# Adaptive layer norm, attention and GEGLU on one core: early bank sharing, the last eight heads as one unit, evictions as tasks, inverse roots on GpSimd

## The chip, the cores and the metric

The kernel runs on one core of a Trainium2 chip. The metric is device time of one execution in microseconds. A core has five engines that run at the same time, each with its own queue of instructions, and meet only at semaphores: TensorE (PE, matrix multiplication; PEld is its loading of weights), VectorE (DVE), ScalarE (ACT, activation functions), GpSimd (POOL) and SyncE (SP, which issues the transfers here). Matrix products land in PSUM, eight banks of 512 fp32 columns in 128 partitions; everything else on chip lies in SBUF.

## The reference

One transformer block: 2048 tokens of 512 numbers, 32 heads of 16, a feed-forward part of 1792, all in bf16. Six vectors (shift, scale and gate of both halves) come from a small vector c.

```python
mod = (silu(c) @ w_mod).reshape(1, 6, 1, -1)
sa, ca, ga, sb, cb, gb = ...
h = layernorm(x) * (1 + ca) + sa
q, k, v = heads of h @ wqkv
p = softmax(q k^T / 4)
x = x + ga * ((p v) @ wo)
h = layernorm(x) * (1 + cb) + sb
x = x + gb * ((gelu(h @ w_gate) * (h @ w_up)) @ w_down)
```

layernorm divides by sqrt(v + 1e-5); gelu is the tanh form.

## The kernel before

**Scores and exponentials.** Scores are computed transposed, keys in the partitions and queries in the columns. A *unit* is a group of heads for one set of query tokens; a *round* of a unit gives four score banks (one for each of four heads, or head pairs), and all banks of all rounds make one long sequence of 2048 positions. `ps_sc` has six banks (`self.scp`), used as two halves of three (CH = 3): even chunks take banks 0 to 2, odd chunks banks 3 to 5. One ACT instruction takes the exponential of the whole chunk (line 1485). In place of the exponential of a bank, DVE can make it by bit arithmetic (`bits`, line 1307): one instruction per bank writes 16-bit patterns, and after four banks of a round (a *quad*) a task of three passes over 128x2048 elements finishes them (`power_task`, line 1574: `mant`, `square`, `expo`). The exponentials are multiplied by V with a column of ones beside it (`pv_mms`), into the one bank `ps_pv`; while the second unit runs (the first two units go through the keys together), bank 5 of `ps_sc` is its accumulator, and odd chunks then have two banks.

**The order is made by a planner.** The Python program records all instructions in one list (`_Recorder.rec`), with a model of when each engine is free, and adds the semaphores. `stream` is a loop that decides at each step what PE does next: a chunk of scores, a round of PV, a step of *side* work, or filler. Sharing a chunk (line 1467) means that one of its three banks goes to DVE; it is allowed if DVE is free early enough (`rule.early`), if a quad can be opened (`new_quad`: two free buffers, not more than `rule.back` waiting DVE steps, V there), and after the keys of group 2 are there. A chunk may also go to DVE entirely (`rule.alone`, line 1449). RULES has a row of nine limits for every 64 positions of the sequence (`SEGB`): ready, hole, back, fill, lag, early, alone, ahead, side2.

**Side work** runs between the chunks: projections of K, Q and V, later for each set of tokens the output projection (`side_wo`), layer norm, and the feed-forward part (`side_ffn`). Each piece fills a bank (`ps_mi`, or bank 5) and is then evicted by DVE. Work on DVE that need not come at once is a *task*: a list of steps under a key, run when the model has DVE free, in the order of `urgency`.

**Units and sets.** The 2048 queries are cut into SETS of 512, 512, 256, 256, 256, 128 and 128 tokens. The first two sets have units of four heads, the later ones of eight heads (n = 2, two heads for each of four row groups). APART names head groups of the last two sets that stay single: for the last set, groups 6 and 7 are two units of four heads and 128 columns. PEN names units whose end is made on DVE alone, without transfers: transposition of 32x32 blocks, reciprocal of the sums, a product, and transposition back (`unit_end`, line 1626).

**Prologue.** `prologue` (line 593) loads x and w_mod, takes mean and variance of four tiles of 128 tokens (tile 1 on ACT), and finds 1/sqrt(v + eps) in eight DVE steps (`ln_rstd_step`: an estimate by integer arithmetic and two Newton steps). Between them DVE makes `sc_bf`, the right operand of the modulation matmuls (`mod_cols`). Then come the norms, PE's transposes, the modulation, the first projections, and the first exponential. POOL makes constants and fills `vaug` (the ones) and `rb`.

**Tail.** The last two sets overlap with the end of attention. For the set before the last, `side_raw` computes gate and up projections in eight chunks (`raw_chunk`), each copied raw out of PSUM by DVE; after the last exponential `tail_rest` applies gelu, product and down projection. `tail_end` does output projection, statistics, inverse root (`ln2_steps`, here six DVE steps), norm, transposes and the feed-forward part of the last tile.

Of the kernel before, what the change touches and what calls it, by code (L numbers as in the profile page):

```python
# [7 lines left out]
ALU = mybir.AluOpType  # L8
# [6 lines left out]
P = 128  # L15
# [18 lines left out]
PEN = {NSET - 2: (6,), NSET - 1: (4, 6, 7)}  # L34
APART = {NSET - 2: (), NSET - 1: (6, 7)}
# [18 lines left out]
def WIN(ends):  # L54
# [8 lines left out]
URGENT = 12  # L63
WUP, WDOWN, WWO, JOIN = (), (), (), 4
# [442 lines left out]
class _Kernel(_Recorder):  # L507
# [12 lines left out]
    def alloc(self):  # L520
# [57 lines left out]
        self.modB = sb("modB", [P, 8], FP32)  # L578
        self.rm4 = self.den[:, 0, 0:4]
# [13 lines left out]
    def prologue(self):  # L593
# [27 lines left out]
        self.memset(pool, self.rm4, Q_SCALE)  # L621
        self.affine_select(self.rm4, [[-32, 4]], ALU.is_ge, 0.0, -16, 1)
# [3 lines left out]
        self.memset(pool, self.vaug[:, :, :].rearrange("p t (h c) -> p t h c", c=VW)[:, :, :, DH:VW], 1.0)  # L626
        self.memset(pool, self.rb[:, :], 0.0)
# [69 lines left out]
    def ln_rstd_step(self, a, b, i):  # L697
# [215 lines left out]
    def ln2_steps(self, k, src=None):  # L913
# [3 lines left out]
        if src is not None:  # L917
            dst = self.normed(k, 0)
            return steps + [lambda h=h: self.ln_norm(a, dst[:, h], src[:, h]) for h in (slice(0, 256), slice(256, D))]
# [916 lines left out]
```

## Time and profile before

| | us |
|---|---|
| median of three runs | 814.53 |
| lowest, highest | 814.52, 815.75 |
| profiled execution, its own time | 814.79 |
| span of the profile | 813.1 |

The granted PE clock is 1.00 in every stage. A profile's row of the timeline gives start, duration (of merged equal instructions together), engine, line, operation, output <- inputs, shapes and count; in brackets the idle time of the engine before it and what ended it. A row of a group gives busy time, mean duration in ns, idle time before. Rows that name L385, L404, L408, L416, L421, L425, L432, L435, L438, L447 and L450 are helpers that record every operation of a kind, so the tiles tell what is what: `E` holds exponentials, `mreg` and `dreg` (among other things) the quads of DVE, `osb` the evicted accumulator, `hreg` the norms and products of the feed-forward part, `xs` the tokens.

### The profile page before, as it was taken

What the parts mean: (1) busy time and instruction counts of PE and PEld (TensorE: products, weight loads), DVE (VectorE), ACT (ScalarE), POOL (GpSimd) and SP (SyncE); (2) the same over time, 40 slices, a digit from 0 to 9 for tenths busy, and PEclk for the clock granted to TensorE, in tenths of its full rate; (3) what the DMA queues carried; (4) which work ended last, traced back from release to release, by engine and by line L of the source; (5) the groups of instructions that cost most, each with busy time, mean ns of one, the idle gap of its engine ahead of it and who ended that gap; (6) DMA issues with size and microseconds to landing.
All of it is one profiled execution on the core that took longest, in us unless ns stands there. A gap on an engine that the chain in (4) does not pass through costs nothing.

```text
span 813.1 us, 28154 instructions
## 1 busy us (share of the span) xinstructions
PE 749.0 (92%) x12749; PEld 289.8 (36%) x12749; DVE 759.8 (93%) x1330; ACT 789.1 (97%) x741; POOL 4.6 (1%) x13
## 2 busy tenths in 40 slices
PE   7899999888898998999989999999989998999998
PEld 3333242322222222222223333333443354345476
DVE  7868999999999999999999999999999999788985
ACT  6999999999999999999999999999999999999993
POOL 2000000000000000000000000000000000000000
PEclk9999999999999999999999999999999999999999
DMA  8100000000001311110003211100554542210000
GB/s 279 60 16 19 13 10 10 10 9 5 11 6 52 95 48 35 45 44 22 16 15 100 62 48 54 48 29 16 153 165 134 167 120 78 72 25 8 20 8 15
DMA packets 70138, 43.53 MB, mean 54 GB/s; under 512 B 15233, under 2 KB 67534, under 8 KB 70018
## 3 DMA queue, kind: packets, MB, share of 16 engines
q1 hardware_dynamic: 70016, 41.73, 18.1%
q8 instruction: 100, 1.64, 0.9%
q14 instruction: 20, 0.16, 0.1%
q10 hardware_dynamic: 2, 0.00, 0.0%
HBM read 39.11 MB, written 2.60 MB: 51 GB/s over the span
## 4 chain that ended last, share of the span: by engine, by line
ACT 66%; PE 20%; DVE 12%; issue 1%; DMA 0%; DVEq 0%
ACT E L404 63%; PE ps_sc L385 10%; PE ps_mi L385 7%; DVE mreg L416 4%; PE ps_pv L385 3%; ACT hreg L404 2%; DVE dreg L416 1%; ACT L404 1%; DVE dreg L408 1%; DVE hreg L425 1%; DVE mreg L408 1%; DVE st L447 1%; DVE hreg L408 0%; DVE osb L425 0%; DVE wreg L408 0%
## 5 line engine op out<-in xcount | busy, mean ns | idle before, releaser
L404 ACT ACTIVATE E<-ps_sc 128x1024 bf16<-128x1024 f32 (+1 forms) x700 | 743.0, 1293 | 4.3 <-PE ps_sc L385 3.9
L385 PE MATMUL ps_sc<-qT,kT 32*128 32x512 bf16 (+2 forms) x2304 | 281.2, 360 | 43.8 <-ACT E L404 37.3
L416 DVE TENSOR_SCALAR mreg<-ps_sc 128x512 uint16<-128x512 f32 x288 | 192.4, 685 | 12.6 <-PE ps_sc L385 10.2
L385 PEld LDWEIGHTS ps_sc<-qT,kT 32*128 32x128 bf16 x2304 | 73.0, 91 | 271.5 <-ACT E L404 227.7
L385 PE MATMUL ps_pv<-E,vaug 128*17 128x256 bf16 (+2 forms) x2696 | 149.2, 292 | 0.1
L385 PE MATMUL ps_mi<-wreg,mreg 128*32 128x512 bf16 (+1 forms) x1760 | 102.0, 330 | 5.1 <-DVE hreg L408 1.9
L416 DVE TENSOR_SCALAR dreg<-ps_sc 128x512 uint16<-128x512 f32 x132 | 88.3, 686 | 2.1 <-PE ps_sc L385 1.1
L416 DVE TENSOR_SCALAR mreg<-mreg 128x2048 uint16<-128x2048 uint16 x113 | 76.5, 683 | 0.3
L385 PEld LDWEIGHTS ps_pv<-E,vaug 128*17 128x17 bf16 x2696 | 54.7, 90 | 59.1 <-issue 43.8
L385 PEld LDWEIGHTS ps_mi<-wreg,mreg 128*32 128x32 bf16 x1760 | 38.5, 95 | 45.0 <-issue 18.1
L385 PE MATMUL ps_pv<-mreg,vaug 128*17 128x256 bf16 (+2 forms) x900 | 49.5, 292 | 1.1 <-DVE mreg L416 0.5
L408 DVE TENSOR_TENSOR mreg<-mreg 128x2048 bf16<-128x2048 bf16 x41 | 49.7, 1212 | 0.1
L385 PE MATMUL ps_pv<-xs,nil 128*17 128x512 bf16 (+1 forms) x584 | 48.4, 375 | 1.1 <-DVE osb L425 1.1
L385 PE MATMUL ps_mi<-hreg,wreg 128*32 128x512 bf16 (+1 forms) x484 | 39.6, 384 | 2.9 <-DVE qT L416 1.6
L425 DVE CAST hreg<-ps_mi 128x512 bf16<-128x512 f32 (+1 forms) x50 | 33.7, 674 | 3.4 <-PE ps_mi L385 2.6
L408 DVE TENSOR_TENSOR dreg<-mreg,dreg 128x2048 bf16<-128x2048 bf16 x29 | 35.1, 1212 | 0.1
L385 PE MATMUL ps_mi<-wo,onorm 128*32 128x512 bf16 x448 | 33.5, 383 | 0.1
L408 DVE TENSOR_TENSOR hreg<-ps_mi,hreg 128x512 bf16<-128x512 f32 x44 | 30.2, 686 | 1.4 <-PE ps_mi L385 0.9
L416 DVE TENSOR_SCALAR dreg<-dreg 128x2048 uint16<-128x2048 uint16 x42 | 28.5, 679 | 0.0
L385 PE MATMUL ps_mi<-mreg,hreg 128*32 128x512 bf16 x352 | 28.3, 385 | 0.0
L408 DVE TENSOR_TENSOR mreg<-dreg,mreg 128x2048 bf16<-128x2048 bf16 x23 | 28.0, 1218 | 0.0
L385 PE MATMUL ps_pv<-dreg,vaug 128*17 128x256 bf16 (+2 forms) x468 | 27.3, 296 | 0.4 <-DVE dreg L408 0.2
(166 smaller groups left out, 616.5 us busy)
## 6 DMA issues: line engine op xcount, KB each, us to landing
mreg<-in_B_w_gate_dram SPq DMA_DIRECT2D x28, 256.0 KB, 3.5
mreg<-in_B_w_up_dram SPq DMA_DIRECT2D x28, 256.0 KB, 2.8
mreg<-in_B_w_down_dram SPq DMA_DIRECT2D x16, 256.0 KB, 2.8
rb<-scr_rec SPq DMA_DIRECT2D x116, 32.0 KB, 1.8
dreg<-in_B_w_down_dram SPq DMA_DIRECT2D x12, 256.0 KB, 5.1
mreg<-in_w_mod_dram SPq DMA_DIRECT2D x1, 2048.0 KB, 13.2
out_dram<-xs SPq DMA_DIRECT2D x15, 128.0 KB, 1.7
xs<-in_A_x_dram SPq DMA_DIRECT2D x3, 512.0 KB, 6.1
```

The lines of the kernel that those rows point to most:

```text
L385: return self.rec("pe", lambda e: e.matmul(out, lhsT, rhs, start=start, stop=stop, tile_position=tp), [lhsT, rhs, *after], [out], cost=(n, ...
L404: return self.rec("act", lambda e: e.activation(out, in_, func, scale=scale, **kw), rd, wr, cost=self.cost("act", out, [in_], "act") + load)
L408: return self.rec(eng, lambda e: e.tensor_tensor(out, a, b, op), [a, b], [out], cost=self.cost(eng, out, [a, b], "tt"))
L416: return self.rec(eng, lambda e: e.tensor_scalar(out, a, s1, s2, **kw), rd, [out], cost=self.cost(eng, out, [a], "ts") + (60 if len(rd) > ...
L425: return self.rec(eng, lambda e: e.tensor_copy(out, in_), [in_], [out], cost=self.cost(eng, out, [in_], "ts"))
L447: return self.rec("dve", lambda e: e.bn_stats(out, in_), [in_], [out], cost=self.cost("dve", out, [in_], "bn"))
```

## The change

Four edits of the order of work and of where it is done, and new numbers in the limits.

- Odd chunks: while bank 5 of `ps_sc` would come free more than 60 ns (by the planner's model) after bank 3 and the present time, near the end of the first two units, an odd chunk takes two banks instead of waiting for three. Up to position 128 (`ODDL`) a two-bank chunk may be shared too: one bank to ACT and one to DVE. Chunks of DVE alone keep to that number of banks.
- The last set: APART is empty, so its head groups 6 and 7 are one unit of eight heads and 256 columns, in PEN as group 6.
- The eight raw evictions become tasks of urgency 0 (`RAWU`), with at most two of them open.
- The inverse roots of the first four tiles, and of the last tile, are two instructions on GpSimd: an addition of eps and a power of -0.5, for which a small tile `mhalf` is filled. The two memsets of `vaug` and `rb` on GpSimd come after the first of these, and the two DVE steps that make `sc_bf` no longer stand between steps of the root. The loop of the tail also steps tasks of GpSimd.
- RULES: 27 of the 32 rows have other numbers.

```diff
-PEN = {NSET - 2: (6,), NSET - 1: (4, 6, 7)}
-APART = {NSET - 2: (), NSET - 1: (6, 7)}
+PEN = {NSET - 2: (6,), NSET - 1: (4, 6)}
+APART = {NSET - 2: (), NSET - 1: ()}
...
+RAWU = 0
+ODDG, ODDL = 9999, 128
+ODDE = 0
...
-    (80, 50, 10, 4200, 1536, 1100, 2500, 20, 700),
...
+    (80, 200, 10, 4200, 2560, 0, 2500, 24, 700),
...
-    (30, 200, 8, 3600, 1024, 850, 4000, 24, 3200),
...
+    (30, 200, 4, 3600, 1024, 850, 1300, 24, 700),
...
         self.memset(pool, self.rm4, Q_SCALE)
+        self.memset(pool, self.mhalf, -0.5)
...
-        self.memset(pool, self.vaug[:, :, :].rearrange("p t (h c) -> p t h c", c=VW)[:, :, :, DH:VW], 1.0)
-        self.memset(pool, self.rb[:, :], 0.0)
...
         self.warm_up(10)
-        for i in range(self.RSTD):
-            self.ln_rstd_step(0, 4, i)
-            if i == 2:
-                self.stt(self.tcol[:, :], self.tcol[:, :], 1.0, self.scp[:, 0, 0:NDC], ALU.add, ALU.mult)
-            elif i == 4:
-                self.ts(dve, self.sc_bf[:, :], self.tcol[:, :], 0.5, None, ALU.mult)
+        self.ln_rstd_pool(0, 4)
+        self.memset(pool, self.vaug[:, :, :].rearrange("p t (h c) -> p t h c", c=VW)[:, :, :, DH:VW], 1.0)
+        self.memset(pool, self.rb[:, :], 0.0)
+        self.stt(self.tcol[:, :], self.tcol[:, :], 1.0, self.scp[:, 0, 0:NDC], ALU.add, ALU.mult)
+        self.ts(dve, self.sc_bf[:, :], self.tcol[:, :], 0.5, None, ALU.mult)
...
+    def ln_rstd_pool(self, a, b):
+        x, y = self.nwx[:, a:b], self.rstd[:, a:b]
+        self.ts("pool", x, self.mv[:, a:b, 1], EPS, None, ALU.add)
+        self.tt("pool", y, x, self.mhalf[:, 0:b - a], ALU.pow)
...
+            steps = [("pool", lambda: self.ts("pool", x, self.mv[:, a:b, 1], EPS, None, ALU.add)),
+                     ("pool", lambda: self.tt("pool", y, x, self.mhalf[:, 0:1], ALU.pow))]
...
     def side_raw(self, k):
         for i in range(NRAW):
+            if i > 1:
+                yield from self.until(("raw", k, i - 2))
             f = yield from self.raw_chunk(k, i, self.bank())
-            f("dve")
-            self.done(("raw", k, i))
+            if not self.dry:
+                self.task([lambda f=f: f("dve")], ("raw", k, i))
             yield END
+        for i in range(2):
+            yield from self.until(("raw", k, NRAW - 1 - i))
...
-            mem, after = take(CH - 1 if (left[units[1]] or self.two) and c % 2 else CH)
+            nb = CH - 1 if (left[units[1]] or self.two) and c % 2 else CH
+            if nb == CH and c % 2 and pos < nsplit + 48:
+                x, y = (self.probe(lambda: self.mm(self.scp[:, i, 0:P], *filler)) for i in (SC - 1, CH))
+                if x > max(y, t) + 60:
+                    nb = CH - 1
+            mem, after = take(nb)
...
-                if len(mem) == CH and ("k", 2, 0) in self.have and self.free["dve"] < max(t + 400, self.free["act"]) + self.rule.early:
+                if (len(mem) == CH or len(mem) == nb and (pos >= ODDG or pos < ODDL)) and ("k", 2, 0) in self.have and (
+                        self.free["dve"] < max(t + 400, self.free["act"]) + self.rule.early - (CH - nb) * ODDE):
...
-                    mem, after = take(CH - 1)
+                    mem, after = take(nb - 1)
```

More of the change, by code (lines that the diff above doesn't have):

```diff
@@ L578, in alloc @@
         self.modB = sb("modB", [P, 8], FP32)
+        self.mhalf = sb("mhalf", [P, 4], FP32)[:, :]
         self.rm4 = self.den[:, 0, 0:4]
@@ L918, in ln2_steps @@
             dst = self.normed(k, 0)
+            x, y = self.nwx[:, a:b], self.rstd[:, a:b]
+            steps = [("pool", lambda: self.ts("pool", x, self.mv[:, a:b, 1], EPS, None, ALU.add)),
+                     ("pool", lambda: self.tt("pool", y, x, self.mhalf[:, 0:1], ALU.pow))]
             return steps + [lambda h=h: self.ln_norm(a, dst[:, h], src[:, h]) for h in (slice(0, 256), slice(256, D))]
@@ L1103, in urgency @@
             return -2
+        if tk[1] is not None and tk[1][0] == "raw":
+            return RAWU
         if tk[1] is None or tk[1][0] in ("st2", "ln2", "den", "onorm"):
@@ L1281, in pick @@
         def pick(q):
-            used = [seq[m][2] for m in take(CH - 1)[0]]
+            used = [seq[m][2] for m in take(nb - 1)[0]]
             return next((q["rnd"][2] + j for j in q["j"] if j not in used), None)
@@ L1450, in stream @@
                     alone = []
-                    while len(alone) < CH:
+                    while len(alone) < nb:
                         if quad is None and not new_quad(overdue()):
@@ L1472, in stream @@
                     elif new_quad(hot):
-                        mem, after = take(CH)
+                        mem, after = take(nb)
                         g = pick(quad)
                 if g is not None:
-                    mem, after = take(CH - 1)
+                    mem, after = take(nb - 1)
                 items = [(m, s0 + i) for i, m in enumerate(mem)]
@@ L1674, in tail @@
             t = self.pe_now()
-            while any(self.step(x, max(self.free[x], t) + 40) for x in ("act", "dve", "sp")):
+            while any(self.step(x, max(self.free[x], t) + 40) for x in ("act", "dve", "pool", "sp")):
                 pass
@@ L1750, in tail_end @@
         yield from self.until(("ln2", k))
-        assert not self.work
+        while self.work:
+            yield None
         for dc in range(NDC):
```

50 rows, old and new, of the table RULES are left out of this document.

## The prediction

> **What bounds the kernel now.** First the page: its span and busy line, the chain that ended last, and the groups that carry the softmax exponentials.
>
> ```profile
> span 813.1 us, 28154 instructions
> PE 749.0 (92%) x12749; PEld 289.8 (36%) x12749; DVE 759.8 (93%) x1330; ACT 789.1 (97%) x741; POOL 4.6 (1%) x13
> ...
> ACT 66%; PE 20%; DVE 12%; issue 1%; DMA 0%; DVEq 0%
> ...
> L416 DVE TENSOR_SCALAR mreg<-ps_sc 128x512 uint16<-128x512 f32 x288 | 192.4, 685 | 12.6 <-PE ps_sc L385 10.2
> ...
> L416 DVE TENSOR_SCALAR dreg<-ps_sc 128x512 uint16<-128x512 f32 x132 | 88.3, 686 | 2.1 <-PE ps_sc L385 1.1
> L416 DVE TENSOR_SCALAR mreg<-mreg 128x2048 uint16<-128x2048 uint16 x113 | 76.5, 683 | 0.3
> L408 DVE TENSOR_TENSOR mreg<-mreg 128x2048 bf16<-128x2048 bf16 x41 | 49.7, 1212 | 0.1
> ```
>
> ScalarE (ACT) is the bound, with VectorE (DVE) and TensorE (PE) close behind. The scores come as 512-column banks of PSUM: DVE turned 288 + 132 = 420 of them into powers by bit arithmetic, ACT the rest. Next the shapes of ACT's exponentials and its timeline, which merges equal work.
>
> ```profile
> L404 ACT ACTIVATE E<-ps_sc 128x1024 bf16<-128x1024 f32 x460 | 452.4, 1151 | 1.5 <-PE ps_sc L385 1.2
> L404 ACT ACTIVATE E<-ps_sc 128x1536 bf16<-128x1536 f32 x236 | 344.6, 1582 | 1.2 <-PE ps_sc L385 1.1
> ```
> ```profile
> 13.63 28.57 ACT L404 ACTIVATE E<-ps_sc 128x1536 bf16<-128x1536 f32 x25 [0.58 <-PE ps_sc L385]
> ...
> 61.91 11.47 ACT L404 ACTIVATE E<-ps_sc 128x1536 bf16<-128x1536 f32 x11 [0.53 <-PE ps_sc L385]
> 74.18 232.78 ACT L404 ACTIVATE E<-ps_sc 128x1024 bf16<-128x1024 f32 x217 [0.80 <-PE ps_sc L385]
> ...
> 792.08 1.28 ACT L404 ACT_TABLE_LOAD   x1
> ```
>
> One bank more in an ACT instruction costs 1582 - 1151 = 431 ns. From 13.63 to 792.08 ACT hardly rests; the last pause of note is the 0.80 us before 74.18. So the execution has three parts: a head of 13.6 us before the first exponential, 778 us of ACT work, and a tail of 21 us. In the middle, time is won only by banks that go from ACT to DVE or by pauses that go away. Whether DVE can take more is read from busy time by stage.
>
> ```profile
> 42.50:74.20 31.70, 29.68 (x544) 11.14 (x543) 22.47 (x40) 30.29 (x31) 0.31 (x1) 1.00 0.08 20
> 74.20:692.00 617.80, 569.03 (x9063) 200.39 (x9065) 606.95 (x990) 617.57 (x565) 0.00 (x0) 1.00 0.20 54
> 692.00:792.10 100.10, 97.60 (x2429) 50.84 (x2420) 86.12 (x161) 99.77 (x99) 0.00 (x0) 1.00 0.10 25
> ```
>
> The columns are the stretch, its length, and then busy time of PE, weight loads, DVE, ACT and POOL (GpSimd). DVE is idle 9.23 us of the first stretch, 10.85 us (1.8%) of the long second, 13.98 us of the third, where PE has only 2.50 us left. A bank on DVE costs 0.685 us for the bits and a quarter of three passes over four banks, (0.683 + 1.212 + 0.683)/4 = 0.64; together 1.33 us, for 0.43 us of ACT.
>
> **The change, part by part.**
>
> *The wait for the accumulator bank (removes a wait).* While the second unit runs, the sixth score bank is its accumulator and odd chunks have two banks. The first odd chunk after it asks for three, so all its matmuls stand behind the second copy here:
>
> ```profile
> 41.41 0.69 DVE L425 CAST kT<-ps_mi 128x512 bf16<-128x512 f32 x1 [1.57 <-PE ps_mi L385]
> ...
> 72.97 0.69 DVE L425 COPY osb<-ps_sc 128x512 f32<-128x512 f32 x1
> ```
>
> It ends at 73.66 and ACT starts 0.5 us later, after its 0.80 us pause. The new test looks when that bank comes free and takes two banks if it is late. Worth 0 to -0.8; I take -0.7, since ACT's row names this very wait. What is late next is the same bank one chunk on, after the copy has ended.
>
> *Odd chunks of two banks shared early (moves banks to DVE).* Up to position 128 such a chunk may now give one bank to DVE. Sharing still waits for the keys of group 2 (first row above, done at 42.1), so this acts in the stretch from 42.50 to 74.20. Its 9.23 us of DVE idleness hold 9.23/1.33 = 6.9 banks, or -3.0 us. The other end is above nothing: DVE also evicts the K, Q and V projections there, PE refills their one bank only after that, and a bank of bits ahead of an eviction delays it by 0.69 us; one such delay that reaches ACT gives +0.7. I take three banks, 3 x 0.43 = -1.3, under half of what the idleness holds, because PE at 29.68 of 31.70 us and the two pauses of ACT (0.53 and 0.80) show that the projections press too.
>
> *Inverse roots of the first tiles by a power on GpSimd.* Head of the kernel, rows of the timelines and of the tile that holds the first part of w_mod:
>
> ```profile
> L457 SPq DMA_DIRECT2D mreg<-in_w_mod_dram x2: 462/484/507, 1.8 to 2.3; - x2
> ...
> DMA to landing us min/median/max: 6.1/6.6/7.1
> ```
> ```profile
> 1.70 0.45 POOL L438 TENSOR_SCALAR_AFFINE_SELECT den<-den 128x4 f32<-128x4 f32 x2
> 2.08 2.27 POOL L435 MEMSET vaug<- 128x512 bf16 x1
> 6.08 0.18 DVE L450 BATCH_NORM_AGGREGATE mv<-st 128x2 f32<-128x6 f32 x1
> 7.18 0.16 DVE L416 TENSOR_SCALAR sc_bf<-tcol 128x4 bf16<-128x4 f32 x1
> 7.89 0.16 DVE L421 SCALAR_TENSOR_TENSOR nwt<-mv,rstd 128x4 f32<-128x4 f32 x1
> 7.97 1.05 DVE L416 TENSOR_SCALAR dreg<-xs,mv,rstd 128x512 bf16<-128x512 bf16 x3
> 8.05 0.54 PE L385 MATMUL ps_sc<-sc_bf,mreg 128*128 128x1 bf16 x16 [0.75 <-DVE nwt L421]
> 9.10 0.61 PE L389 MATMUL ps_sc<-ident,dreg 128*128 128x128 bf16 x8
> 57.68 0.17 DVE L435 MEMSET self<- 128x128 f32 x1
> 57.99 0.31 POOL L438 TENSOR_SCALAR_AFFINE_SELECT self<-self 128x128 f32<-128x128 f32 x1 [52.78 <-DVE self L435]
> ```
>
> Eight DVE steps fall away between 6.26 and 7.86. In their place: a hop to POOL (57.85 to 57.99: 0.14), an add, a power, a hop back. POOL's nearest rows of 128x4 take 0.45/2 = 0.23 each; the power is not in the trace. Its lower bound is 0.23; from above I use the largest POOL rate here, 2.27 us for 512 columns or 18 ns for four columns, a generous forty times over: 0.7. I take 0.4, nearer the 128x4 row because that has its shape. The norms could start near 7.2 instead of 7.97. But PE decides: its first modulation matmuls need 1.81 + 6.1 = 7.91 at the least for w_mod to land, and start at 8.05, though their other operand was ready at 7.34. From there PE works without a gap into the transposes, which need the first norm by 9.10. So the earlier root buys 0, and up to about 0.6 us of lateness would be hidden as well. The two memsets, moved behind the power, have until the first V eviction, which comes after the first exponential.
>
> [...]
>
> *Last eight heads as one unit.* The tail, with the widths that come in its place:
>
> ```profile
> 792.25 0.32 DVE L432 STREAM_TRANSPOSE osb<-ps_pv 128x128 f32<-128x128 f32 x1
> 792.68 0.85 PE L385 MATMUL ps_pv<-E,vaug 128*17 128x128 bf16 x48
> 794.03 0.32 DVE L432 STREAM_TRANSPOSE osb<-ps_pv 128x128 f32<-128x128 f32 x1 [0.47 <-PE ps_pv L385]
> 795.14 0.31 DVE L432 STREAM_TRANSPOSE onorm<-rb 128x128 bf16<-128x128 bf16 x1
> 795.97 2.75 PE L385 MATMUL ps_pv<-xs,hreg 128*128 128x512 bf16 x12
> 796.35 0.69 DVE L447 BATCH_NORM_STATS2 st<-ps_sc 128x6 f32<-128x512 f32 x1
> 797.07 0.18 DVE L450 BATCH_NORM_AGGREGATE mv<-st 128x2 f32<-128x6 f32 x1
> 798.57 0.99 DVE L416 TENSOR_SCALAR E<-ps_sc,mv,rstd 128x256 bf16<-128x256 f32 x2
> ```
> ```profile
> L432 DVE STREAM_TRANSPOSE osb<-ps_pv 128x256 f32<-128x256 f32 x2 | 0.9, 446 | 0.0
> ...
> L408 DVE TENSOR_TENSOR rb<-osb,rden 128x256 bf16<-128x256 f32 x2 | 0.8, 416 | 0.0
> ```
>
> Now the last four heads' PV matmuls begin only when the four before them have left the accumulator: out at 792.57, then 1.3 us of matmuls (48 in 0.85 us, and the DVE banks behind them) up to 794.0. In one unit all but the last round or two can run while ACT still works: last matmul near 793.0, -1.0. The chain after it gets wider: transposition 0.45 for 0.32, product 0.42 for the narrow one's 0.3, and two block transpositions of about 0.3 for one; +0.55, less the 0.39 us raw eviction that stands in it now if that has gone before. Together -0.6 to -1.0: I take -0.8. Bounds 0 (the backlog of PV stays) and -1.2.
>
> *Raw evictions as tasks.* Eight evictions are no longer forced right behind their matmuls; DVE does other work meanwhile, and PE may fill the next chunk, two at most being open. DVE's 13.98 idle microseconds before 792.10 cover them, so 0; bounds -0.4 and +0.4 (one eviction in or out of the last chain).
>
> *The last tile's root.* From 797.25 to 798.57 DVE needs 1.32 us. Instead 0.14 + 0.23 + 0.4 + 0.2 = 0.97: -0.35, between -0.5 and 0 by the bounds of the power. Nothing else waits behind it on POOL.
>
> *What PE gives back.* The fourteenth tile's down matmuls take 0.23 us each from 795.97. If the normalized last tile comes 1.15 us earlier, five of them are not done when its transposes are; PE is the bound of what follows. Some fit into the gaps around the modulation: I take back +0.4.
>
> *The planner's limits (RULES).* They change how many banks DVE takes where, no instruction's price. In the long stretch DVE idles 1.8%, so little is to be won; I take 0, bounds -2.6 and +4.4 (below).
>
> Sum: -0.7 - 1.3 - 0.8 - 0.35 + 0.4 = -2.75. The profiled execution took 814.79 us (span 813.1 and 1.7 around it), 0.26 over the median of 814.53. So 814.53 - 2.75 = **811.8 us**.
>
> **The rivals.**
>
> *The limits cost banks (slower).* Many rows are new: one stretch goes from early 1100 to 0, another's backlog limit from 8 to 4, and DVE gets a bank only when both allow. If DVE's idle share between 74.20 and 692 rose from 1.8% to 4%, that is 13.9 us, 10.4 banks, +4.4: 816.2. It decides from 2.75/0.43 x 1.33 = 8.5 us more idleness (3.1%) on. Against it: other rows raise the same limits, or lower the bar for chunks of DVE alone. Chance 0.13.
>
> *The limits win banks.* A third of the 24.8 idle microseconds after 74.20 holds 6.2 banks, -2.6: 809.2. Against it: after 692 PE is 97.5% busy. Chance 0.18.
>
> *Sharing early buys nothing*, the projections being the bound in that stretch: 811.8 + 1.3 = 813.1. For it: the pauses of ACT there. Chance 0.17.
>
> *The memsets hold the norms up.* Vaug's would run from about 7.1 to 9.4; a first norm after it ends at 9.8, 0.7 behind the transposes' 9.10, and the second memset could meet the other norms. Taking 1.0: 812.8. No SBUF-to-SBUF norm overlaps POOL in the trace, so it is neither borne out nor excluded. Chance 0.08.
>
> [...]
>
> *The power is slow.* At 2 us the tail's root takes 2.57 us for 1.32 and loses 1.25 instead of winning 0.35; in the head the norms start 0.9 later, 0.3 more than is hidden: 811.8 + 1.6 + 0.3 = 813.7. Against it: every POOL row of this shape takes under 0.25 us. Chance 0.04.
>
> **How the numbers follow.** The forecast keeps 0.40. This kernel's measurement tells 0.2%, 1.6 us, from no change: faster is below 812.9, slower above 816.2. Faster: 0.36 of the forecast's 0.40, all 0.18 of the won banks, 0.07 of sharing and 0.05 of the memsets: 0.66. Slower: half of the lost banks and some of mixtures: 0.10. Same: 0.24. The range runs from the won banks with a little more, 809.0, to the lost banks short of their full price, 815.4.
>
> **What would show it.** First exponential still near 13.6 with POOL's power ending before 7.5; no 0.80 us pause of ACT at the end of the split phase; single-bank ACT instructions between 42 and 74 us beside more than 11 DVE banks; one 128x256 block transposition at the end instead of two narrow ones, and statistics of the last tile within 3.5 us of ACT's last exponential instead of 4.3. The number of DVE banks, 420 now, tells the limits. It is wrong if ACT shows new pauses in the long stretch, if that number falls by seven or more, or if the first exponential comes after 14.

## The result, and the profile after

| | before | after |
|---|---|---|
| median of 16 executions each, us | 814.70 | 816.62 |
| lowest, highest | 814.25, 816.14 | 815.72, 818.37 |
| profiled execution, its own time | 814.79 | 816.78 |
| first exponential starts | 13.63 | 18.75 |
| first to last exponential | 778.45 | 775.65 |
| last exponential to the end of the span | 21.02 | 20.70 |

The ratio is 1.0021, 95% interval 1.0013 to 1.0029: slower, by 0.2%. In the profiled executions the head lost 5.12 us, the middle won 2.80, the tail 0.32. (Two executions far off all others, 2769.66 us of the first experiment below and 1525.3 of the kernel before beside it, are left out of the ratios and of the versions' medians.) From the page of after, span and busy line:

```profile
span 815.1 us, 27883 instructions
...
PE 746.0 (92%) x12617; PEld 287.1 (35%) x12617; DVE 764.1 (94%) x1320; ACT 787.6 (97%) x738; POOL 6.7 (1%) x18
```

ACT is as busy as before within 1.5 us (789.1), so the loss is time in which it has nothing to do. Timeline of the head of after:

```profile
6.64 1.05 POOL L411 TENSOR_TENSOR rstd<-nwx,mhalf 128x4 f32<-128x4 f32 x1
7.65 2.28 POOL L438 MEMSET vaug<- 128x512 bf16 x1
...
7.81 3.76 DVE L419 TENSOR_SCALAR dreg<-xs,mv,rstd 128x512 bf16<-128x512 bf16 x3
...
9.52 1.26 POOL L438 MEMSET rb<- 128x1024 f32 x1
...
10.98 0.71 PE L392 MATMUL ps_sc<-ident,dreg 128*128 128x128 bf16 x8 [2.14 <-DVE dreg L419]
...
12.53 0.99 DVE L419 TENSOR_SCALAR hreg<-ps_sc,modA 128x512 bf16<-128x512 bf16 x2 [0.26 <-PE ps_sc L392]
...
13.12 0.29 PE L388 MATMUL ps_pv<-hreg,wreg 128*128 128x128 bf16 x1
...
15.23 1.30 PE L388 MATMUL ps_sc<-hreg,wreg 128*128 128x384 bf16 x4
...
17.97 0.41 PE L388 MATMUL ps_mi<-wreg,hreg 128*32 128x128 bf16 x16 [1.43 <-DVE qT L419]
18.31 0.60 PE L388 MATMUL ps_sc<-qT,kT 32*128 32x512 bf16 x5
...
18.75 1.45 ACT L407 ACTIVATE E<-ps_sc 128x1536 bf16<-128x1536 f32 x1 [2.79 <-PE ps_sc L388]
```

The same stage of before, rows not shown yet; the second memset is the first of them:

```profile
3.95 1.26 POOL L435 MEMSET rb<- 128x1024 f32 x1
...
10.54 0.99 DVE L416 TENSOR_SCALAR hreg<-ps_sc,modA 128x512 bf16<-128x512 bf16 x2 [0.25 <-PE ps_sc L389]
...
11.14 0.23 PE L385 MATMUL ps_pv<-hreg,wreg 128*128 128x128 bf16 x1 [0.15 <-DVE hreg L416]
...
12.38 0.81 PE L385 MATMUL ps_sc<-hreg,wreg 128*128 128x384 bf16 x4
...
13.20 0.40 PE L385 MATMUL ps_sc<-qT,kT 32*128 32x512 bf16 x3
```

Three losses follow one another. **The norms are held**: the three take 3.76 us in place of 1.05, and the modulation comes 12.53 - 10.54 = 1.99 later. **The projections run at half clock**: from the first to the end of the last they take 15.23 + 1.30 - 13.12 = 3.41 us in place of 12.38 + 0.81 - 11.14 = 2.05, another 1.36. **V goes ahead of the scores**: PE waits 1.43 us for an eviction, does 16 V matmuls, and only then the first scores. From the end of the projections to the first exponential it is 18.75 - 16.53 = 2.22 in place of 13.63 - 13.19 = 0.44, 1.78 more. The sum is 5.13, with 5.12 measured. It holds for this execution; the eight of the 16 whose granted clock was 1.00 took 816.2 on average, the seven at 0.998 817.1, so the halved clock is not what carried the time out of the range.

The norms one by one, from the view of their tile (least, median and longest duration in ns), after and then before:

```profile
L419 DVE TENSOR_SCALAR dreg<-xs,mv,rstd x3: 396/402/3116, 7.8 to 11.2; 128x512 bf16<-128x512 bf16 x3
```
```profile
L416 DVE TENSOR_SCALAR dreg<-xs,mv,rstd x3: 404/405/406, 8.0 to 8.6; 128x512 bf16<-128x512 bf16 x3
```

Two keep their 0.40 us; the first takes 3.12. It was issued at 7.81, 0.16 us behind the first memset, and ends at 10.93, just after the second memset (9.52 + 1.26 = 10.78). It was held until about the end of both. The memsets write `vaug` and `rb`, the norm reads `xs`, `mv` and `rstd` and writes `dreg`: it waited for no result of theirs, so in this row the two engines meet at more than semaphores. The second memset, next in GpSimd's queue, ran ahead of the held norm.

The clock, in the windows of after (columns as in the prediction, with the granted clock, the DMA share and GB/s behind them):

```profile
11.00:13.00 2.00, 2.00 (x34) 1.39 (x34) 1.20 (x5) 0.42 (x1) 0.00 (x0) 0.95 0.99 325
13.00:16.00 3.00, 2.89 (x16) 2.05 (x16) 1.00 (x3) 1.78 (x4) 0.00 (x0) 0.50 1.08 344
```

PE had stood still for 2.14 us ahead of 10.98. Two microseconds later, from 12.79 to 16.21, its clock is 0.50, just when the projections need it.

The middle of after, by shape and by stage:

```profile
L407 ACT ACTIVATE E<-ps_sc 128x1024 bf16<-128x1024 f32 x441 | 434.1, 1148 | 0.6 <-PE ps_sc L388 0.4
L407 ACT ACTIVATE E<-ps_sc 128x1536 bf16<-128x1536 f32 x245 | 357.2, 1580 | 3.0 <-PE ps_sc L388 2.8
L419 DVE TENSOR_SCALAR mreg<-ps_sc 128x512 uint16<-128x512 f32 x292 | 195.9, 685 | 8.1 <-PE ps_sc L388 6.1
```
```profile
42.50:74.20 31.70, 30.79 (x540) 11.46 (x540) 27.46 (x50) 31.55 (x33) 0.31 (x1) 1.00 0.08 19
74.20:692.00 617.80, 564.41 (x8976) 197.87 (x8978) 602.91 (x986) 617.09 (x563) 0.00 (x0) 1.00 0.20 53
692.00:794.40 102.40, 99.11 (x2411) 50.96 (x2407) 91.67 (x168) 102.26 (x99) 0.00 (x0) 1.00 0.10 26
```

From 42.50 to 74.20 ACT is idle 0.15 us (1.41 before) and DVE 4.24 (9.23 before): the stage that the edit was to fill is full. Four more banks went to DVE (292 in `mreg` and 132 as before in `dreg`, 424 in all), three of them in this stage (12 for 9). In the long stretch DVE idles 14.89 us, more than the 10.85 of before, and ACT 0.71 against 0.23. From first to last exponential ACT is busy for 774.65 us in place of 776.17 and idle for 1.00 in place of 2.28: of the 2.80 won, 1.52 is ACT's work (four banks at 0.43 would be 1.7) and 1.28 pauses.

The tail of after, from the last exponential (where the table is loaded):

```profile
793.91 1.52 PE L388 MATMUL ps_pv<-E,vaug 128*17 128x128 bf16 x96
795.26 0.62 PE L388 MATMUL ps_pv<-mreg,vaug 128*17 128x128 bf16 x32
...
794.40 1.28 ACT L407 ACT_TABLE_LOAD   x1
...
795.93 0.45 DVE L435 STREAM_TRANSPOSE osb<-ps_pv 128x256 f32<-128x256 f32 x1 [1.00 <-PE ps_pv L388]
...
798.51 0.69 DVE L450 BATCH_NORM_STATS2 st<-ps_sc 128x6 f32<-128x512 f32 x1
799.24 0.18 DVE L453 BATCH_NORM_AGGREGATE mv<-st 128x2 f32<-128x6 f32 x1
800.54 0.99 DVE L419 TENSOR_SCALAR E<-ps_sc,mv,rstd 128x256 bf16<-128x256 f32 x2 [1.12 <-POOL rstd L411]
...
799.82 0.58 POOL L411 TENSOR_TENSOR rstd<-nwx,mhalf 128x1 f32<-128x1 f32 x1
```

The statistics begin 798.51 - 794.40 = 4.11 us after the last exponential, 4.27 before: PV of the last unit, 128 matmuls or eight rounds, begins only 0.49 us ahead of that and ends at 795.88, 1.48 after it (1.89 before). From there to the statistics it is 2.63 us, 2.38 before. From the end of the aggregation (799.42) to the norm it is 1.12 us, 1.32 before; from the norm to the end of the span it is as long as before within 0.1 us (14.56 and 14.53).

### The profile page after: what moved, and what is told of

Read it like the earlier page. It is cut to its first block, busy times and chain, and to the rows that moved or that the text cites. A ratio compares the mean times of both kernels' runs of the same rounds, so it can differ in the third digit from the quotient of the medians.

```text
span 815.1 us, 27883 instructions
## 1 busy us (share of the span) xinstructions
PE 746.0 (92%) x12617; PEld 287.1 (35%) x12617; DVE 764.1 (94%) x1320; ACT 787.6 (97%) x738; POOL 6.7 (1%) x18
## 4 chain that ended last, share of the span: by engine, by line
ACT 79%; PE 15%; DVE 4%; DMA 1%; issue 0%; POOL 0%; POOLq 0%; DVEq 0%; SPq 0%
ACT E L407 76%; PE ps_sc L388 7%; PE ps_mi L388 5%; ACT hreg L407 2%; PE ps_pv L388 2%; ACT L407 1%; DVE mreg L419 1%; DVE dreg L419 1%; DMA mreg<-in_B_w_gate_dram 1%; DVE dreg L411 0%; DVE hreg L411 0%; DMA xs<-in_A_x_dram 0%; DVE st L450 0%; PE ps_sc L392 0%; DVE hreg L419 0%
## 5 line engine op out<-in xcount | busy, mean ns | idle before, releaser
L407 ACT ACTIVATE E<-ps_sc 128x1024 bf16<-128x1024 f32 (+2 forms) x697 | 741.5, 1291 | 5.2 <-PE ps_sc L388 4.8
L388 PE MATMUL ps_sc<-qT,kT 32*128 32x512 bf16 (+1 forms) x2240 | 280.9, 365 | 44.7 <-ACT E L407 38.9
L419 DVE TENSOR_SCALAR mreg<-ps_sc 128x512 uint16<-128x512 f32 x292 | 195.9, 685 | 8.1 <-PE ps_sc L388 6.1
L388 PEld LDWEIGHTS ps_sc<-qT,kT 32*128 32x128 bf16 x2240 | 71.3, 91 | 272.6 <-ACT E L407 231.6
L419 DVE TENSOR_SCALAR mreg<-mreg 128x2048 uint16<-128x2048 uint16 x117 | 79.3, 683 | 0.2
L388 PE MATMUL ps_pv<-mreg,vaug 128*17 128x256 bf16 (+2 forms) x940 | 52.0, 291 | 2.2 <-DVE mreg L411 1.1
L411 DVE TENSOR_TENSOR mreg<-mreg 128x2048 bf16<-128x2048 bf16 x44 | 53.4, 1215 | 0.1
L388 PE MATMUL ps_pv<-xs,nil 128*17 128x512 bf16 (+1 forms) x496 | 42.4, 375 | 0.5 <-DVE nwx L419 0.3
L411 DVE TENSOR_TENSOR hreg<-ps_mi,hreg 128x512 bf16<-128x512 f32 x47 | 32.2, 685 | 0.9 <-PE ps_mi L388 0.7
```

Of the source, the lines that this page charges most:

```text
L388: return self.rec("pe", lambda e: e.matmul(out, lhsT, rhs, start=start, stop=stop, tile_position=tp), [lhsT, rhs, *after], [out], cost=(n, ...
L407: return self.rec("act", lambda e: e.activation(out, in_, func, scale=scale, **kw), rd, wr, cost=self.cost("act", out, [in_], "act") + load)
L411: return self.rec(eng, lambda e: e.tensor_tensor(out, a, b, op), [a, b], [out], cost=self.cost(eng, out, [a, b], "tt"))
L419: return self.rec(eng, lambda e: e.tensor_scalar(out, a, s1, s2, **kw), rd, [out], cost=self.cost(eng, out, [a], "ts") + (60 if len(rd) > ...
```

## The experiments

Medians stand against those of the kernel before, measured beside them (814.77 for the first five, then 815.04, 814.81 and 815.05). Where only a single execution was made, the profile's sections are compared.

A first exponential read from one profile has a scatter of its own. The versions with the memsets behind the norms and the changed row 0 of RULES share one head, and in six profiles theirs comes between 14.91 and 16.48, in step with the first modulation matmuls, which start between 7.26 and 9.12; in three of the six their row names the transfer of w_mod as what they waited for. Counted from that start, the first exponential comes 7.35 or 7.36 us later in five of the six, and 5.58 later in the kernel before: the 1.8 us of V ahead of the scores stand clear of the scatter.

### The head

**The memsets behind the norms, the rest of the changed kernel in its own order.**

```diff
-        self.memset(pool, vaug ones, 1.0)
-        self.memset(pool, self.rb[:, :], 0.0)
...
+        self.memset(pool, vaug ones, 1.0, after=(self.tb1[:, 0, 3, :],))
+        self.memset(pool, self.rb[:, :], 0.0, after=(self.tb1[:, 0, 3, :],))
         self.act(self.modA[:, 0:4], self.scp[:, 1, 0:4], ACT.Copy)
```

> The changed kernel with one more wait: GpSimd's two memsets start only when the norms of the first four tiles are done; the order of instructions is the same on every engine. Theory (a memset on GpSimd holds up VectorE's norms, bf16 from SBUF to SBUF): the three norms take about 1.05 us again instead of 3.76, the transposes start near 9.1 instead of 10.98, PE's granted clock stays at 1.00, and the first exponential comes 1.99 + 1.38 = 3.4 us earlier, near 15.4; time 816.6 - 3.4 = 813.2. Rival (the power itself is what costs, 1.05 us on GpSimd): nothing changes, 816.6, first exponential at 18.7. Rival (the modulation and its evictions are held up in the same way): the loss moves to the modulation, first exponential at 17 or later.

```profile
L419 DVE TENSOR_SCALAR dreg<-xs,mv,rstd x3: 408/409/411, 7.8 to 8.4; 128x512 bf16<-128x512 bf16 x3
```
```profile
8.89 2.28 POOL L438 MEMSET vaug<- 128x512 bf16 x1 [1.23 <-DVE dreg L419]
...
8.99 0.61 PE L392 MATMUL ps_sc<-ident,dreg 128*128 128x128 bf16 x8
...
10.43 0.99 DVE L419 TENSOR_SCALAR hreg<-ps_sc,modA 128x512 bf16<-128x512 bf16 x2 [0.25 <-PE ps_sc L392]
...
14.52 0.41 PE L388 MATMUL ps_mi<-wreg,hreg 128*32 128x128 bf16 x16 [1.43 <-DVE qT L419]
...
15.29 1.45 ACT L407 ACTIVATE E<-ps_sc 128x1536 bf16<-128x1536 f32 x1 [2.35 <-PE ps_sc L388]
```

The norms have their 0.41 us again while the memsets run behind them, the first projections start 2.09 us earlier and run at full clock (1.36), and the first exponential comes at 15.29, 3.46 earlier. First to last exponential: 775.74 us, as in the changed kernel. The times fall in two groups: 813.39 to 813.64 at a granted clock of 1.00 (three executions) and 814.99 to 816.53 at 0.996 (eight); median 815.37, ratio 1.0003 (0.9994 to 1.0012). The mechanism is right, the forecast met in the first group only: in most executions the clock falls. PE's wait of 1.43 us ahead of V is still there, but that this wait is the cause is not shown: five other versions with the same head, one execution each, ran at 0.999 or 1.00.

**The reverse: the kernel before, its memsets made to wait for the inverse roots** (`after=(self.rstd[:, 0:4],)`, nothing else).

> The kernel before the change, with GpSimd's two memsets made to wait for the inverse root on VectorE; no power, no other part of the change. Theory (memsets beside the norms): norms end only with the memsets near 11.2, PE pauses 2 us, its clock falls, first exponential near 17.3 instead of 13.63; time 814.6 + 3.7 = 818.3. Rival (the power, or the new order of the first matmuls, is what costs): 814.6, first exponential at 13.6.

```profile
L416 DVE TENSOR_SCALAR dreg<-xs,mv,rstd x3: 395/402/3210, 8.2 to 11.6; 128x512 bf16<-128x512 bf16 x3
```

Median 818.32, ratio 1.0044 (1.0029 to 1.0060), as forecast. The one move costs the old kernel 3.55 us, with the same single norm of 3.2 us, and without any power. The profile is of one of the two slowest executions (820.49, clock 0.994); its first exponential comes at 18.23, 0.9 later than forecast. The two executions at clock 1.00 took 816.93 and 816.97, about 2.2 more than before: that is the hold without the clock.

**Ten more dummy matmuls while PE waits for the norms**, everything else as changed.

```diff
         self.warm_up(WARM[0])
+        self.warm_up(10)
```

The ten are not in the planner's model, so nothing else moves.

> The changed kernel with ten more dummy matmuls of 512 columns (2.2 us) on PE in the place where it waits for the norms; all else in the same order. Theory (the pause of PE, not anything else, halves its clock afterwards): norms and transposes as late as before (3.76 us, 10.98), but the granted clock stays at 1.00 and the first projections take 2.05 instead of 3.43 us; first exponential near 17.4, time 815.2. Rival (the clock falls for another reason, or its loss is hidden behind VectorE): clock and time as in the changed kernel, 816.6.

The clock stays 1.00 in the head and the first exponential comes at 17.58, 1.17 earlier; median 816.04, ratio 1.0017 (1.0009 to 1.0026). In the profiled execution the clock was worth 1.36 us, less the 0.2 by which the dummies themselves delay the projections. The medians differ by 0.6 only, and their intervals overlap: eight of 16 executions of the changed kernel are at 1.00 too, here nine of 12.

**The memsets back in their old place**, ahead of everything.

> The changed kernel with the two memsets back in their old place, before the power. Theory: norms 1.05 us, first exponential between 13.6 (if the V matmuls that now stand ahead of the first scores cost nothing without the delay) and 15.4 (if they cost their 1.75 us); with the 2.8 us that the changed kernel wins between first and last exponential, time 811.5 to 813.2. Rival (the gains in the middle exist only in the model of the planner): 814 or more.

A miss: median 818.93, ratio 1.0049 (1.0032 to 1.0066). The planner saw other times and put its filler elsewhere:

```profile
15.54 0.83 PE L388 MATMUL ps_sc<-xs,ident 128*32 128x512 bf16 x12 [0.53 <-DMA xs<-in_A_x_dram]
```
```profile
16.00:19.00 3.00, 3.00 (x63) 1.44 (x55) 1.54 (x5) 2.27 (x3) 0.00 (x0) 0.60 1.06 364
19.00:22.00 3.00, 2.74 (x25) 0.49 (x23) 2.72 (x13) 2.01 (x3) 0.00 (x0) 0.50 1.03 411
```

Twelve fillers wait for a tile of x that has not landed, with the second chunk of scores behind them; the clock is halved from 16.61 to 23.44. The first exponential came at 15.06, as the theory wanted, and first to last took 780.6. An edit of this program is only clean if the order is held fast; the versions that follow in this section take the changed kernel's recorded order and move named instructions in it.

**Scores ahead of V:** the memsets in their old place, the first 16 V matmuls behind the first five score matmuls.

> The changed kernel in its own order, with two moves: the two memsets of GpSimd back before the power, and the first 16 V matmuls behind the first five score matmuls instead of ahead of them. Theory (the new order puts V matmuls, which need a bank that VectorE still reads, ahead of the first scores; PE stands for 1.4 us, and in most executions its clock is halved after that): first exponential near 13.5 instead of 15.29, no pause of PE over 1 us before it, granted clock 1.00 in nearly all executions; time 813.4 (the undisturbed executions of the run with late memsets) - 1.75 = 811.7, with a spread under 1 us. Rival (the loss only moves on, since the V products are now later): ACT pauses soon after its first exponentials, 813 or more.

```profile
13.38 4.80 ACT L418 ACTIVATE E<-ps_sc 128x1536 bf16<-128x1536 f32 x4 [0.58 <-PE ps_sc L399]
...
18.15 0.39 PE L399 MATMUL ps_pv<-E,vaug 128*17 128x512 bf16 x4 [1.30 <-DVE vaug L439]
...
19.13 2.36 ACT L418 ACTIVATE E<-ps_sc 128x1536 bf16<-128x1536 f32 x2 [0.94 <-PE ps_sc L399]
```

The first exponential is at 13.38, so the order brings it forward by the 1.9 us. In the profile all of that comes back: PV waits for `vaug`, the next scores stand behind PV, ACT pauses 0.94 us (and 0.35 at 21.85), and from first to last exponential it is 777.89 us in place of 775.74. This execution and the one of the memsets behind the norms, both at clock 1.00, end within 0.2 us of each other. What is better is the clock: eight of 12 executions are at 1.00, there three of 11. Median 813.62, ratio 0.9990 (0.9980 to 1.0000): **the lowest median measured**, 3.0 us under the changed kernel, but not clear of no change against the one before. The rival, that the loss only moves on, was right.

**The first V eviction sooner, and the next three score matmuls ahead of the transposes**, on top.

> Same order as the version with the first five score matmuls ahead of the V matmuls and the memsets early, with two further moves. The first eviction of V to vaug goes ahead of the statistics of the last two tiles (VectorE, two pairs of 0.66 + 0.18 us), and the three score matmuls of the next chunk go ahead of the eight transposes of the second tile group. Theory (the pauses of ScalarE of 0.94 us at 19.1 and 0.35 us at 21.9 are PE standing behind PV matmuls that wait for vaug, and behind transposes that wait for norms): vaug lands near 16.5 in place of 18.1, both pauses go, last exponential near 790.0 after a first one at 13.4, median 812.4 (813.6 - 1.3), faster than before by about 0.28%. Rival (the middle has room, what is won at the start is waited for at the next projection, as the five-score version already gave back 2.1 us of its 1.9): a new pause of 0.5 us or more before 45 us, first to last exponential stays at 777.9, median 813.4 or more.

```profile
18.00:21.00 3.00, 1.86 (x17) 0.72 (x13) 2.46 (x11) 3.00 (x3) 0.00 (x0) 1.00 1.01 404
21.00:24.00 3.00, 2.98 (x26) 1.14 (x23) 1.57 (x4) 1.39 (x2) 0.00 (x0) 0.51 0.47 182
```

The two old pauses are gone, but PE, ahead of its work, stood still in 18 to 21 (1.86 busy of 3.00), its clock fell to 0.51, and ACT paused 1.00 and 1.39 us later on. Median 815.38, ratio 1.0009 (0.9998 to 1.0020). So the rival has its new pauses; the clock, which neither theory had named, is a candidate for their cause.

**That gap filled.**

> The version before it with the three score matmuls moved up (its PE stood still for 0.63 us at 18.5 to 19.2, its granted clock then was 0.51 from 21 to 24, and ScalarE paused 1.00 and 1.39 us), plus eight more dummy matmuls that add zeros to the accumulator, placed in that gap. Theory (the clock falls because of the gap): clock 1.00 from 18 to 27, the two pauses go or shrink under 0.4 together, median 813.0 or less and runs with granted clock 1.00. Rival (the clock falls for another reason, or the pauses come from the order): clock under 0.9 in a stretch between 19 and 27 again, median 815.4 as before the edit.

The program of this run held none of the eight matmuls, so it is the one above measured again: median 816.02, and the lowest execution 812.77 at clock 1.00. With them in it:

> The version with the memsets early, five score matmuls ahead of V, the first V eviction sooner and three score matmuls moved up, and now really with eight more dummy matmuls (zeros added to the accumulator) in PE's gap of 0.63 us at 18.5 to 19.2. That version without them: medians 815.38 and 816.02 in two measurements, executions from 812.77 at granted clock 1.00 to 818.52 at 0.994. Theory (the clock falls because PE stands still there): most executions at 0.999 or 1.00, median 812.8 to 813.3, faster than before by about 0.2%. Rival (the clock falls with other gaps or by chance): granted clocks from 0.994 to 0.998 in most executions, median 815 to 816, a stretch of 0.5 between 21 and 27 in the profile.

```profile
18.00:21.00 3.00, 2.58 (x30) 0.71 (x27) 2.65 (x14) 3.00 (x4) 0.00 (x0) 1.00 1.04 404
21.00:24.00 3.00, 2.37 (x25) 1.39 (x28) 1.38 (x4) 2.07 (x2) 0.00 (x0) 0.84 0.79 307
24.00:27.00 3.00, 3.00 (x26) 0.53 (x27) 0.99 (x2) 1.45 (x1) 0.00 (x0) 0.59 0.02 5
```
```profile
22.58 1.02 ACT L418 ACTIVATE E<-ps_sc 128x1024 bf16<-128x1024 f32 x1 [0.54 <-PE ps_sc L399]
```

Eight of 11 executions are at 1.00, in the two runs without the matmuls 3 of 24. Median 814.31, ratio 0.9990 (0.9981 to 0.9999). The gap was a cause of the lost clock, not the only one: in this profile the clock falls two microseconds later (at 23.06), after PE's next waits. Nor is the clock the only cause of the pauses: ACT pauses 0.54 us ahead of 22.58, still at full clock, and 1.94 ahead of 25.54. The forecast of 812.8 to 813.3 was not reached, and at clock 1.00 the executions average 813.9, with 813.3 for the version that only puts the scores first: the earlier eviction of V won nothing.

### The middle

Each is a single execution. **No early sharing** (`ODDL = 0`), **the old RULES**, and **no bank test** (`if False:`), each in the kernel with the memsets behind the norms; and **the new RULES alone** in the kernel before.

> The changed kernel with memsets after the norms, and odd chunks of two banks never shared. From the first to the last exponential the changed kernel takes 775.65 us, the one before 778.45. Theory (the 2.8 us come mostly from sharing early: seven single-bank instructions of ACT between 42 and 74 us): 775.65 + 7 x 0.43 = 778.7 at most, over 777 in any case. Rival (they come from the pause before the accumulator bank and from the new limits): under 776.5.

> The changed kernel with the memsets behind the norms, and the RULES of before. Its reference has 775.7 us from first to last exponential, the kernel before 778.45. Theory (prediction's: early sharing and the bank test win 2.0, the limits nothing): 776.5 from first to last, first exponential 13.5 (scores ahead of V, as fill is 3900 again), 813.7 - 1.8 + 0.8 = 812.6 in all. Rival (the limits carry the gain of the middle): 778.4, in all 814.5. If it is over 780 the limits are fitted to the rest of the order, and neither can be read from it. Either way it tells whether V goes ahead of the scores by row 0 of RULES.

> The changed kernel with the memsets behind the norms, and without the test that gives an odd chunk two banks while the accumulator bank comes free late. Reference: 775.7 us from first to last exponential, no pause of ScalarE between 42.5 and 74.2 beyond 0.15. Theory (prediction's: the test is worth 0.7): a pause of 0.5 to 0.8 before the first three-bank odd chunk, near 72 to 74 us, and 776.4 from first to last. Rival (the limits or sharing have moved that spot already): no such pause, 775.7. Over 779 the order has changed elsewhere too and only the pause can be read.

> The kernel before with the changed kernel's RULES alone (old prologue, memsets early, no early sharing, no bank test, last heads apart). Theory (prediction's: the limits win nothing by themselves): first to last exponential 778.5, first exponential about 15.2 since row 0 sets V ahead of the scores, 816.3 in all. Rival (the limits carry the gain of the middle): 776, 814 in all. Over 781: limits and edits are fitted to each other, and the gain of the middle belongs to the pair only.

| | first exponential | first to last | time |
|---|---|---|---|
| changed, memsets behind the norms | 15.29 | 775.7 | 813.5 |
| no early sharing | 15.70 | 785.8 | 826.8 |
| old RULES | 13.66 | 787.0 | 822.9 |
| no bank test | 15.33 | 782.0 | 820.2 |
| new RULES in the kernel before | 14.84 | 786.9 | 826.9 |

All four are 6 to 11 us longer in the middle than their kernel, beyond every theory; for the last three it was put down ahead that such a time would mean a changed order, or limits fitted to the rest. In all four DVE takes 412 banks, twelve fewer than in the changed kernel and eight fewer than in the one before; at 0.43 us a bank that is 3.4 to 5.2 us more work for ACT (4.6 to 6.6 measured). The rest is idle time of ACT, about 4 to 5 us in three of them. Two of them also lose 2.4 to 3 us in the tail. That the limits, one row for every 64 positions, no longer fit the shifted order is the likely reason, not a shown one. So how much of the 2.8 us limits and edits each carry stays open. Two readings stand. Row 0 of RULES decides the order of V and the scores: with the old row scores come first, and the first exponential is at 13.66; with the new row in the old kernel V comes first. Which of the seven changed numbers of that row does it was not tested. And the pause that the prediction named is still there with the new limits alone:

```profile
74.32 11.53 ACT L404 ACTIVATE E<-ps_sc 128x1024 bf16<-128x1024 f32 x12 [0.82 <-PE ps_sc L385]
```
```profile
15.33 70.67 ACT L407 ACTIVATE E<-ps_sc 128x1536 bf16<-128x1536 f32 x67 [2.35 <-PE ps_sc L388]
```

The second row is the version without the bank test: 67 exponentials from 15.33 to 86.0 without a pause (from 42.50 to 74.20 ACT idles 0.20 us). Its theory, a pause of 0.5 to 0.8, falls. The version without early sharing, with the test, has none either from 40 to 95: in these orders each of the two removes the pause without the other, so the 0.7 of the test is no separate term beside early sharing.

### The tail

A single execution each, in the kernel with the memsets behind the norms (last exponential to span end 811.7 - 791.03 = 20.67, to the statistics 4.11).

**The last eight heads apart again** (PEN and APART of before).

> The changed kernel with memsets after the norms, and the last eight heads again as two units of four; nothing else differs before the last sets. Theory of the prediction (one unit wins 0.8): from ACT's last exponential to the end of the span 21.5 us instead of 20.7. Rival (the last PV matmuls end no earlier, since PE is full, and the wider chain eats the rest, as the traces suggest with 4.27 and 4.11 us from the last exponential to the statistics): 20.7 to 20.9.

The span ends 21.43 after the last exponential, the statistics begin 4.86 after it: the one unit is worth 0.76 in this schedule. PV of the last unit ends 2.71 us after the last exponential there, 1.48 with one unit, so 1.23 is won at that end, and the wider chain gives 0.48 back.

**The last root on DVE again.**

> The changed kernel with memsets after the norms, and the inverse root of the last tile on VectorE in six steps again. Theory: from the end of the aggregation to the start of the norm 1.32 us instead of 1.12, so the span after ACT's last exponential is 0.2 longer. Rival (PE has other work to do meanwhile): no difference in the span, the down matmuls of the other tile take its place.

From the start of the aggregation (796.66) to the norm (798.15) it is 1.49 us in place of 1.31, and the span ends 20.77 after the last exponential: GpSimd is worth 0.18 there, 0.10 at the end.

**Raw evictions inline.**

> The changed kernel with the memsets behind the norms, and the eight raw evictions inline behind their matmuls as in the kernel before (the order differs only late). Reference: last exponential 791.0, statistics of the last tile end 4.11 us after it, span end 20.67 after it. Theory (as predicted, the tasks are worth nothing): last exponential within 0.4 of 791.0 and statistics within 0.4 of 4.1 after it. Rival (the tasks keep the eviction out of the last chain): statistics 0.4 to 0.7 later. Second rival (the tasks delay PV at the end): statistics at least 0.5 sooner, near 3.5.

```profile
791.42 1.02 ACT L407 ACTIVATE E<-ps_sc 128x1024 bf16<-128x1024 f32 x1 [0.84 <-PE ps_sc L388]
...
795.90 0.69 DVE L450 BATCH_NORM_STATS2 st<-ps_sc 128x6 f32<-128x512 f32 x1
```

The second rival is half right: the statistics begin 3.44 us after the last exponential (which ends at 792.46), 0.67 sooner, but the last exponential waits 0.84 us for PE. From the first exponential (16.00) to the statistics it is 779.90, with tasks 779.85: worth nothing, only moved.

## Why the prediction was wrong, point by point

- **Forecast: 811.8, and 816.62 came, outside the range.** The parts without the head give -2.80 - 0.32 = -3.1, near the forecast's -2.75, in part by luck: the middle won more than its terms and the tail less. The head, forecast at nothing, gave +5.1.
- **The step that failed first is "the earlier root buys 0, and up to about 0.6 us of lateness would be hidden".** The root was not late: GpSimd's power ended at 7.69 and the norms were issued at 7.81, before the 7.97 of before. What was late was the first norm's execution, blocked by the memsets moved behind the power. "The two memsets ... have until the first V eviction" looked at who needs their result, not at whom they hold up while they run. The floor under that step was not firm either: w_mod did not need until 7.91, its matmuls start at 7.63 in the changed kernel and at 6.89 in the earliest profile.
- **The rival "the memsets hold the norms up" had the mechanism, a chance of 0.08, and 1.0 us.** The norm waited for both memsets, not for the first: 1.99. And the price did not end there: PE stood still for 2.14 us and its clock fell behind that, 1.36 more in the profiled execution. Both memsets had rows in the profile of before, 2.27 and 1.26 us, and the end of the two in a row was the time to take for the first norm.
- **"RULES ... I take 0" failed in the head.** The prediction weighed the limits for the long stretch only. The new row 0 set V ahead of the first scores: 1.8 us later for the first exponential. The version with the scores first shows that the middle gives such a gain back, so what of it the whole time bears stays open. Of the marks of being wrong, a first exponential after 14 was the one that showed it (18.75).
- **The bank wait (-0.7) and early sharing (-1.3):** the pause is gone, there are single-bank exponentials, and DVE has 12 banks there for 9, the three that were taken; its idleness fell by 5 us. -2.0 was forecast for the middle, -2.8 measured (1.52 of work, 1.28 of pauses), with the limits' share in it unknown. The rival that the limits cost banks did not come: 424 for 420.
- **One unit, -0.8:** its own terms, -1.0 + 0.55 and at best another -0.39, give -0.45 to -0.84 and not -0.6 to -1.0. Measured, it is 0.76 against heads apart within the changed schedule, but against before PV ended only 0.41 sooner behind the last exponential and the chain took 0.25 longer: 0.16. "All but the last round or two can run while ACT still works" was wrong: 128 PV matmuls ran from 793.91 to 795.88, mostly after it, and the mark of 3.5 us became 4.11. The tail as a whole won 0.32, where -0.75 was forecast for its three terms; of the +0.4 that PE was to take back nothing came.
- **The power, 0.4 (0.23 to 0.7):** 1.05 us for 128x4 and 0.58 for 128x1; the first lies outside the bounds, which were made from memsets and selections. The last root won 0.20, not 0.35.
- **Raw evictions, 0:** right.

## What to carry to other kernels

When an instruction is moved to a time at which its engine is "free", look at what the neighbour does then: two memsets, 3.5 us together, that stood beside loads and statistics before, made a 0.4 us norm take 3.1. Before costing a delay at its own length, see what PE does meanwhile: here a wait of 2.14 us was followed by 3.42 us at a clock of 0.50, and the work behind it took 1.36 us longer; a few dummy matmuls in the gap are cheap (0.2 us here). A planner with fitted limits cannot be tested by switching one part off; replay its recorded order and move single instructions instead.

## What the hardware showed that was not expected

- GpSimd's memsets held up a bf16 norm from SBUF to SBUF (3.12 us for 0.40 in the changed kernel, 3.21 in the reverse experiment), but not VectorE reading PSUM: in the version with the memsets behind the norms the memsets run from 8.89 to 12.01 beside the two modulations, which take 0.54 us each, 0.99 together, as in the kernel before.
- The clock fell for one of two lengths of time. In the six profiles in which it falls in the head, the stretch at 0.50 lasts 3.42 us (changed kernel, 12.79 to 16.21) or twice that (reverse experiment, 10.76 to 17.58), three times each. In the 3.42 us ahead of the fall PE was not idle: it was busy for 1.2 to 2.4 us, and in the version with the V eviction sooner its longest wait there is 0.63 us. What sets the time of the fall is not shown.
- The granted clock of executions comes mostly in steps of 0.002, which by estimate is 0.002 x 813 / 0.5 = 3.3 us at half speed, about one such stretch of 3.42. Each step costs about 1.5 us in the program with the V eviction sooner, measured again (812.77 and 814.06 at 1.00, 814.4 to 816.1 at 0.998, 816.0 to 816.5 at 0.995 and 0.996, 818.03 at 0.994), 0.9 in the changed kernel. So a head with short waits of PE has several times, and one execution does not show which.
